# Chunk 0's attention products in halves, and a new written order, in a one-core transformer block

## The chip, the cores and the metric

The kernel runs on one core of a Trainium2 chip. The metric is the device time of one execution in microseconds. A core has five engines that run their own queues side by side: PE (TensorE, matrix products and transposes), DVE (VectorE), ACT (ScalarE), POOL (GpSimd) and SP (SyncE, here only issuing DMAs). POOL and ACT issue DMAs too. Each engine takes its instructions in the order in which the program lists them and waits on semaphores for what other engines or DMAs produce.

## The reference: what is computed

The input x has 2048 positions of 512 values, in bf16. One block is computed:

```python
h = x + A_ref(layernorm(x), wqkv, wo)      # attention
out = h + B_ref(layernorm(h), W_gate, W_up, W_down)   # gated MLP, relu(gate) * up, 1376 wide
```

The attention has 32 heads of 16 values. Each position looks at eight positions only: itself and those 2, 4, ... 14 before it. So for each position and head there are eight scores `q . k / 4`, a softmax over these eight (positions before the start are masked), and a sum of eight `weight * v`. The result goes through `wo`.

## The kernel before, in words

**Chunks.** The 2048 positions are four chunks of 512 (`CS`), named 0 to 3 (`tk`). Data is kept transposed: channels on the 128 partitions, 512 positions along the free side, four tiles of channels (`t` = 0 to 3). A tile named `quad` holds four channel tiles of one chunk (normalized x, q, attention output, normalized h); a tile named `big` holds 8 x 512 values; a `bank` is one of eight accumulators of PE; a `row` is 128 positions of x or h before they are transposed.

**The steps of a chunk.**

1. *Layernorm of x* (lines 397 to 514). DVE takes the statistics (L431, L434), ACT forms the factor with Ln and Exp (L444, L448), DVE normalizes 128 positions at a time into a `row` (L466). The row is transposed by PE (L495) and copied out of the bank by ACT (L511) or, for two rows of chunk 0, by DVE (L509); or, for those in the list `DMAT` (line 348), by a DMA transpose that SP issues (L484). All of chunk 3's x goes that last way.
2. *q, k, v* (lines 529 to 562). Twelve groups of four matmuls (one for each slice of 128 of the contraction), L536, each copied out by ACT (L544). Chunk 0's first four groups (q and k of tiles 0 and 1) are split by positions: the first 256 columns after two transposed rows, the other 256 after the other two.
3. *Scores* (lines 565 to 629). For each half `hf` of the window (four offsets) and each pair of channel tiles, one DVE instruction forms `q * k` for two tiles, four offsets and 512 positions (L583, 128x4096). PE adds up the 16 values of a head with the matrix `sel` (L589, 16 matmuls for each half), ACT takes the exponential (L619), and for chunk 0 DVE masks the start (L622).
4. *Weights* (lines 632 to 697). PE sums the denominators (L639), ACT inverts them by Ln and Exp (L642, L645). In chunks 1 to 3 DVE multiplies the weights by the inverse at once (L663); in chunk 0 the result is divided at the end (L717). The weights are spread over the channels: for chunks 0 and 1 by PE (L689) and eight copies by ACT (L695), for chunks 2 and 3 by eight DMA broadcasts from SP (L679).
5. *Weighted sum* (lines 700 to 751). For each channel tile one DVE instruction forms `weight * v` for all eight offsets (L710, 128x4096). The eight are added in a tree. For chunks 0 to 2 (`DACC`) the first level, four onto four, is an accumulating DMA that POOL issues (L742); the other levels are DVE (L713, 1024 and 512 wide).
6. *Output product and residual* (lines 756 to 782): `wo` on PE (L762); in chunk 0 PE adds x too (L765) and ACT writes the sum (L771), otherwise DVE does it (L773).
7. *Layernorm of h*, with the same helper: squares on ACT (L420), factor on ACT (L441, L448), rows on DVE (L466), transposes.
8. *MLP* (lines 787 to 864): 11 column tiles of up and gate on PE (L800), copied out by ACT (L804, L807), multiplied by DVE (L820), the down product on PE (L837), the last addition on DVE (L848), the store by SP (L854).

**What sets the order.** The kernel does not issue these steps as it walks over the chunks. Each call of `add` (lines 102 to 111) records a step: engine, an estimated duration, what it depends on, which buffers it takes. The list `RANK` (lines 18 to 56) gives each recorded step a number; for each engine the steps go in the order of these numbers (lines 125 to 129). `Plan.order` (lines 116 to 188) places the steps of all engines on one time line with the estimated durations and then issues them by start time, so the estimates decide how engines' steps interleave in the program and which of the shared buffers a step gets, and `RANK` decides the order within an engine. Estimated landing times of the loads are in lines 377 to 379, those of DMA queues in the `dq` of a step (lines 169 to 172).

**The loads** (lines 290 to 321) are not part of the plan and are the same before and after: chunk 0's x, the four slices of the q/k weights (two from SP, two from ACT), chunk 1's x, the v weights, and then the rest.

Of the kernel before, what the change touches and what calls it, by code (L numbers as in the profile page):

```python
# [55 lines left out]
]  # L56


class Op:

# [31 lines left out]
class Plan:  # L92
# [23 lines left out]
    def order(self):  # L116
# [14 lines left out]
        while left:  # L131
# [27 lines left out]
            for eng, cands in best.items():  # L159
# [5 lines left out]
                if pick is None or t < pick[0]:  # L165
                    pick = (t, op)
            t, op = pick
            op.start, op.done = t, t + op.dur + op.lat
            if op.dq:
                at = max(t + op.dur + op.dq[0], free.get("DQ", 0.0)) + op.dq[1]  # L170
                free["DQ"] = at
                op.done = at + op.lat
# [734 lines left out]
```

## Time and profile before

| | |
|---|---|
| time, median of 3 runs | 200.8 us (200.71 to 200.93) |
| the profiled execution's own time | 201.23 us |
| its span, first to last instruction | 199.5 us |
| granted clock of TensorE | 1.000 |
| PE busy | 191.6 us, 96% |
| DVE busy | 152.6 us, 77% |
| ACT busy | 115.0 us, 58% |
| POOL busy | 12.6 us, 6% |

A row of a timeline begins with the start and the length in us from the span's start, then the engine, the line of the kernel, the operation, what is written and read, the shape and a count (x4: four such instructions, merged), and in brackets the idle time of the engine before it and what ended it. A row of the chain of waits has start, length, and what the chain went through. A row of the waits view reads: engine and line, what it waited for, us in total, how often, the longest. A group's row ends with busy us, mean ns of one, and idle us before. A row of the windows view gives, after the stretch, its length and the busy us (and counts) of PE, PE's weight loads, DVE, ACT and POOL, then clock, DMA share and GB/s.

### The profile page before, as it was taken

To read this page: it belongs to the slowest core of one execution; us is meant where nothing else is said; L and a number is where in the kernel's file an instruction comes from. 1 tells how busy PE (TensorE), PEld (TensorE's weight loads), DVE (VectorE), ACT (ScalarE), POOL (GpSimd) and SP (SyncE) were. 2 spreads that over 40 slices of the span, in tenths; PEclk is the share of its full clock that TensorE was granted. 3 is DMA by queue.
4 is the path that set the end of the run, shared out by engine and by line. 5 is a ranking of instruction groups with operands and counts; after the bars stand their busy time and mean duration, and the time that the engine had idled before them with its cause. 6 is when DMAs were issued, how large, how long until landed. Compare 5 with 4: busy or idle time off the path is not lost.

```text
span 199.5 us, 2918 instructions
## 1 busy us (share of the span) xinstructions
PE 191.6 (96%) x1080; PEld 95.7 (48%) x1099; DVE 152.6 (77%) x239; ACT 115.0 (58%) x240; POOL 12.6 (6%) x28
## 2 busy tenths in 40 slices
PE   8599999999999999999999999999999999999994
PEld 8385445554445344444444444444444444444542
DVE  6669999999999999998899859999964423032332
ACT  3455899881999987663844557701439620456500
POOL 4000000330000004100113000000000000000000
PEclk9999999999999999999999999999999999999999
DMA  6959981897000008985269970140010130102022
GB/s 166 327 185 324 412 283 32 156 192 148 3 0 0 3 0 157 190 165 123 39 118 196 208 204 2 26 85 20 3 53 0 26 79 0 31 0 79 0 79 79
DMA packets 19981, 20.92 MB, mean 105 GB/s; under 512 B 8608, under 2 KB 16768, under 8 KB 19968
## 3 DMA queue, kind: packets, MB, share of 16 engines
q1 hardware_dynamic: 17520, 13.60, 23.0%
q0 software_dynamic: 1728, 6.29, 16.8%
q10 hardware_dynamic: 720, 0.85, 1.6%
q8 instruction: 8, 0.13, 0.3%
q14 instruction: 5, 0.04, 0.1%
HBM read 8.42 MB, written 2.10 MB: 53 GB/s over the span
## 4 chain that ended last, share of the span: by engine, by line
PE 91%; DMA 4%; ACT 2%; issue 1%; SPq 1%; DVE 0%
PE bank L800 37%; PE bank L536 21%; PE bank L837 19%; PE bank L762 7%; DMA wqk_sb<-in_A_wqkv_dram 4%; PE bank L589 3%; PE bank L495 2%; ACT big L695 1%; PE bank L639 1%; ACT quad L511 1%; PE bank L765 0%; SPq L292 0%; PE bank L689 0%; ACT quad L544 0%; SPq L294 0%
## 5 line engine op out<-in xcount | busy, mean ns | idle before, releaser
L800 PE MATMUL bank<-quad,wu_sb 128*128 128x512 bf16 (+1 forms) x170 | 42.7, 379 | 0.7 <-ACT quad L511 0.3
L800 PE MATMUL bank<-quad,wg_sb 128*128 128x512 bf16 (+1 forms) x173 | 41.6, 379 | 0.1
L837 PE MATMUL bank<-wd_sb,gT 128*128 128x512 bf16 (+3 forms) x184 | 39.4, 366 | 0.2
L807 ACT ACTIVATE gr<-bank 128x512 bf16<-128x512 f32 (+1 forms) x44 | 25.3, 601 | 23.3 <-PE bank L800 21.8
L804 ACT CAST up_sb<-bank 128x512 bf16<-128x512 f32 (+1 forms) x44 | 25.1, 588 | 23.2 <-PE bank L800 22.4
L710 DVE TENSOR_TENSOR big<-big,vT 128x4096 bf16<-128x4096 bf16 x16 | 36.1, 2290 | 0.8 <-DMA big<-ex 0.6
L583 DVE TENSOR_TENSOR big<-quad,kT 128x4096 bf16<-128x4096 bf16 x16 | 36.2, 2288 | 0.4 <-ACT quad L544 0.4
L536 PE MATMUL bank<-quad,wqk_sb 128*128 128x512 bf16 (+1 forms) x140 | 30.3, 356 | 2.1 <-DMA wqk_sb<-in_A_wqkv_dram 1.8
L820 DVE TENSOR_TENSOR gT<-gr,up_sb 128x1024 bf16<-128x1024 bf16 (+1 forms) x24 | 15.2, 646 | 20.5 <-ACT up_sb L804 10.4
L837 PEld LDWEIGHTS <-gT 128*128 128x128 bf16 (+1 forms) x187 | 18.2, 98 | 19.7
L800 PEld LDWEIGHTS <-wu_sb 128*128 128x128 bf16 (+1 forms) x176 | 17.5, 100 | 21.1 <-issue 1.3
L800 PEld LDWEIGHTS <-wg_sb 128*128 128x128 bf16 (+1 forms) x176 | 17.6, 100 | 20.5 <-issue 0.2
L536 PEld LDWEIGHTS <-wqk_sb 128*128 128x128 bf16 x144 | 15.5, 114 | 14.3 <-DMA wqk_sb<-in_A_wqkv_dram 2.3
L848 DVE TENSOR_TENSOR row<-x_sm,bank 128x512 bf16<-128x512 bf16 (+1 forms) x17 | 10.8, 653 | 10.6 <-PE bank L837 10.6
L713 DVE TENSOR_TENSOR big<-big 128x1024 bf16<-128x1024 bf16 (+2 forms) x24 | 17.2, 735 | 0.7 <-DMA big<-big 0.6
L742 POOL DMA_DIRECT2D big<-big x12 | 10.5, 872 | 86.8 <-DVE big L710 42.7
L536 PE MATMUL bank<-quad,wv_sb 128*128 128x512 bf16 x62 | 15.2, 380 | 0.1
L762 PE MATMUL bank<-wo_sb,quad 128*128 128x512 bf16 x63 | 15.2, 379 | 0.1
L466 DVE TENSOR_SCALAR row<-x_sm,mv,rs 128x512 bf16<-128x512 bf16 x32 | 11.6, 407 | 2.3 <-ACT rs L448 2.1
L431 DVE BATCH_NORM_STATS2 st<-x_sm 128x6 f32<-128x512 bf16 x16 | 10.5, 680 | 3.4 <-DMA x_sm<-in_A_x_dram 3.4
L420 ACT ACTIVATE row<-x_sm,mv 128x512 bf16<-128x512 bf16 x12 | 8.6, 723 | 5.0 <-DVE mv L412 5.0
L544 ACT CAST kT<-bank 128x512 bf16<-128x512 f32 x16 | 9.2, 592 | 3.4 <-PE bank L536 3.4
(68 smaller groups left out, 141.6 us busy)
## 6 DMA issues: line engine op xcount, KB each, us to landing
big<-big POOLq DMA_DIRECT2D x12, 512.0 KB, 5.5
big<-ex SPq DMA_DIRECT2D x16, 128.0 KB, 2.8
out_dram<-row SPq DMA_DIRECT2D x15, 128.0 KB, 1.8
x_sm<-in_A_x_dram SPq DMA_DIRECT2D x3, 512.0 KB, 6.4
wu_sb<-in_B_W_up_dram SPq DMA_DIRECT2D x1, 1376.0 KB, 9.7
wg_sb<-in_B_W_gate_dram SPq DMA_DIRECT2D x1, 1376.0 KB, 12.7
wd_sb<-in_B_W_down_dram SPq DMA_DIRECT2D x1, 1280.0 KB, 15.7
wqk_sb<-in_A_wqkv_dram ACTq DMA_DIRECT2D x2, 256.0 KB, 7.2
```

The lines of the kernel that those rows point to most:

```text
L466: V.tensor_scalar(out=xn.t[:], in0=x, scalar1=mv.t[:, j, 0:1], scalar2=rs.t[:, j:j + 1], op0=ALU.add if residual else ALU.subtract, op1=AL ...
L536: nc.tensor.matmul(mm.t[:, lo:hi], lhsT=wv_sb[:, dt, t:D:NT] if c == 2 else wqk_sb[:, dt, c * D + t:(c + 1) * D:NT], rhs=xnT.t[:, dt, lo:h ...
L583: V.tensor_tensor(out=pb.t[:].rearrange("p (t w) s -> p t w s", t=2), in0=q4, in1=k4, op=ALU.mult)
L710: V.tensor_tensor(out=mt.t[:], in0=ab.t[:], in1=v8, op=ALU.mult)
L713: V.tensor_tensor(out=mt.t[:, 0:n, :], in0=mt.t[:, 0:n, :], in1=mt.t[:, n:2 * n, :], op=ALU.add)
L762: nc.tensor.matmul(od.t[:], lhsT=OT.t[:, t, j * P:(j + 1) * P], rhs=wo_sb[:, t, :], start=(t == 0), stop=(t == NT - 1 and tk not in RPE))
L800: nc.tensor.matmul(mm.t[:fs, :], lhsT=w_sb[:, dt, ft * P: ft * P + fs], rhs=hnT.t[:, dt, :], start=(dt == 0), stop=(dt == NT - 1))
L804: nc.scalar.copy(out=ub.t[:fs, i, :], in_=um.t[:fs, :])
L807: nc.scalar.activation(out=gr.t[:fs, i, :], in_=gm.t[:fs, :], func=ACT.Relu)
L820: V.tensor_tensor(out=gt.t[:fs, 0:n, :], in0=gr.t[:fs, 0:n, :], in1=ub.t[:fs, 0:n, :], op=ALU.mult)
L837: nc.tensor.matmul(od.t[:, c0:c1], lhsT=gts[ft].t[:fs, ft % 2, j * P:(j + 1) * P], rhs=wd_sb[:fs, ft, c0:c1], start=(ft == 0), stop=(ft == ...
L848: V.tensor_tensor(out=ob.t[:, c0:c1], in0=x_sm[:, tk * BPC + j, c0:c1], in1=od.t[:, c0:c1], op=ALU.add)
```

## The change

Five things change in what is issued.

1. **q*k of chunk 0 in halves** (`PRS = (0,)`). Each of the four DVE instructions of L583 becomes two, one for each channel tile (128x2048). Each half depends on the q and k of its own tile alone. PE's sums still come as one step of 16 matmuls after all four halves of a window half.
2. **weight*v of chunk 0 in halves** (`MUH = (0,)`). Each of the four DVE instructions of L710 becomes two, one for each window half; the first depends on the first four weight copies alone. The accumulating DMA still follows both.
3. **The first four q/k groups of chunk 0.** Before: 256 columns, all four slices of the contraction, then the other 256. After: 256 columns with slices 0 and 1, the other 256 with slices 0 and 1, and then all 512 columns with slices 2 and 3. A group is 4 + 2 matmuls in place of 8. The steps on slices 0 and 1 have a load of their own (`ab`) to wait for in the plan.
4. **The plan's estimates.** Later landing times for the loads, and a finer model of DMA queues: accumulating transfers (POOL) share one queue, DMA transposes and broadcasts that meet one of them are planned as slowed.
5. **A new `RANK`**: 735 numbers in place of 722, so the order on every engine is new.

The change's own description adds that chunk 3's DMA transposes are ordered ahead of chunk 0's accumulating transfers. Other options that the code gains (`PRD`, `DAC2`, `HSP`) are empty and issue nothing.

```diff
-    0, 1, 2, 3, 4, 5, ... 720, 721,
+    0, 1, 2, 3, 4, 5, ... 733, 734,
...
+    PRS, MUH = (0,), (0,)
...
-    xload = [[load(t) for t in (3.5, 3.7, 4.1, 4.35)]] + [[load(t)] * BPC for t in (9.15, 13.2, 15.4)]
+    xload = [[load(t) for t in (3.5, 3.7, 4.1, 4.35)]] + [[load(t)] * BPC for t in (10.8, 14.4, 17.8)]
...
-             (("q", 7.78), ("k", 7.78), ("v", 10.6), ("o", 17.1), ("u", 20.5), ("g", 24.0), ("d", 28.5))}
+             (("q", 9.55), ("k", 9.55), ("ab", 8.1), ("v", 12.1), ("o", 19.2), ("u", 22.6), ("g", 26.1), ("d", 30.1))}
...
-                a = None
+                ab, done = [wload["ab"]], []
                 for i, (lo, hi, evs) in enumerate(((0, 2 * P, xev[0:2]), (2 * P, CS, xev[2:]))):
-                    a = add(("qk%s%d" % ("ac"[i], n), tk), "PE", 4 * MM * (hi - lo) / CS + 0.02,
-                            lambda f=f_mm, lo=lo, hi=hi: f(lo, hi), evs + [wl, a, fills[-1]], pr - 5, take=[mm],
-                            use=[xnT], lat=PEL if i == 1 else 0.0)
+                    done.append(add(("qk%s%d" % ("ac"[i], n), tk), "PE", 2 * MM * (hi - lo) / CS + 0.005,
+                                    lambda f=f_mm, lo=lo, hi=hi: f(lo, hi, 0, 2), evs + ab + done + [fills[-1]], pr - 5,
+                                    take=[mm], use=[xnT]))
+                a = add(("qkd%d" % n, tk), "PE", 2 * MM, lambda f=f_mm: f(0, CS, 2, NT), done + [wl], pr - 4.9, take=[mm],
+                        use=[xnT], lat=PEL)
...
+                if tk in PRS:
+                    def f_p1(u, t=t, hf=hf, pb=pb, qT=qT, s0=s0):
+                        kb = kT[:, t + u, PADL + s0 - 4 * hf * DIL: PADL + s0 - 4 * hf * DIL + CS]
+                        k4 = bass.AP(tensor=kb.tensor, offset=kb.offset,
+                                     ap=[list(kb.ap[0]), [-DIL, 4]] + [list(y) for y in kb.ap[1:]])
+                        V.tensor_tensor(out=pb.t[:, 4 * u:4 * u + 4, :],
+                                        in0=qT.t[:, t + u, :].unsqueeze(1).to_broadcast([P, 4, CS]), in1=k4, op=ALU.mult)
+
+                    for u in range(2):
+                        a = add(("pr%d%s" % (hf, "ac"[u]), tk), "DVE", D20, lambda u=u, f=f_p1: f(u),
+                                [d[t + u] for d in (qd, kd, kp)], apr, take=[pb], use=[qT], lat=DL)
+                        prd.append((a, pb, f_sc if u else lambda: None))
...
+            if tk in MUH:
+                def f_m1(hf, t=t, ab=ab, mt=mt, s0=s0):
+                    vb = vT[:, t, PADL + s0 - 4 * hf * DIL: PADL + s0 - 4 * hf * DIL + CS]
+                    v4 = bass.AP(tensor=vb.tensor, offset=vb.offset,
+                                 ap=[list(vb.ap[0]), [-DIL, 4]] + [list(y) for y in vb.ap[1:]])
+                    V.tensor_tensor(out=mt.t[:, 4 * hf:4 * hf + 4, :], in0=ab.t[:, 4 * hf:4 * hf + 4, :], in1=v4, op=ALU.mult)
+
+                ms = [add(("mu%d%s" % (t, "ac"[hf]), tk), "DVE", D20, lambda hf=hf, f=f_m1: f(hf),
+                          [x for x in abd if x.key[0][2] == str(hf)] + vds, tpr, take=[mt], use=[ab], lat=DL) for hf in range(2)]
```

More of the change, by code (lines that the diff above doesn't have):

```diff
@@ L168, in order @@
             op.start, op.done = t, t + op.dur + op.lat
+            held = 0.0
             if op.dq:
-                at = max(t + op.dur + op.dq[0], free.get("DQ", 0.0)) + op.dq[1]
-                free["DQ"] = at
+                at, sw, busy = t + op.dur + op.dq[0], free.get("DQ", 0.0), op.dq[1]
+                if op.eng == "POOL":
+                    late = 1.0 if at < free.get("DT", -1.0) + 0.3 else 0.0
+                    at = free["DQ"] = max(at, sw) + late + busy
+                else:
+                    turn = 0.6 < busy < 0.9
+                    at = max(at, free.get("DQ" + op.eng, 0.0))
+                    if at < sw + (0.3 if turn else 0.0):
+                        share = 0.03 if turn else 0.18
+                        late = max(sw - at, 0.0)
+                        at += busy / share if late * share >= busy else late + busy - late * share
+                        free["DQ"] = sw + (1.65 if turn else 0.5 * busy)
+                        held = at + op.lat - 4.5
+                    else:
+                        at += busy
+                    free["DQ" + op.eng] = at
+                    if turn:
+                        free["DT"] = at
                 op.done = at + op.lat
-            free[op.eng] = t + op.dur
+            free[op.eng] = max(t + op.dur, held)
             for b in op.take:
@@ L216 @@
     PRE = ()
+    PRD = ()
     NAB = 0
@@ L532, with f_mm @@
             pr = base + 10 + 0.1 * n
-            def f_mm(lo=0, hi=CS, c=c, t=t, mm=mm, xnT=xnT):
-                for dt in range(NT):
+            def f_mm(lo=0, hi=CS, d0=0, d1=NT, c=c, t=t, mm=mm, xnT=xnT):
+                for dt in range(d0, d1):
                     nc.tensor.matmul(mm.t[:, lo:hi], lhsT=wv_sb[:, dt, t:D:NT] if c == 2 else wqk_sb[:, dt, c * D + t:(c + 1) * D:NT],
-                                     rhs=xnT.t[:, dt, lo:hi], start=(dt == 0), stop=(dt == NT - 1))
+                                     rhs=xnT.t[:, dt, lo:hi], start=(dt == 0 and lo == 0), stop=(dt == NT - 1))
             def f_ev(c=c, t=t, mm=mm, qT=qT, s0=s0):
@@ new lines, with f_pd, f_sc @@
+            if (tk, hf) in PRD:
+                def f_pd(p0=prd[0][1], p1=prd[1][1]):
+                    nc.gpsimd.dma_start(p0.t[:], p1.t[:], accum_op=ALU.add, max_dma_last_dim=4096)
+                a = add(("pd%d" % hf, tk), "POOL", 1.3, f_pd, [a for a, _, _ in prd], apr, use=[b for _, b, _ in prd],
+                        lat=1.1, dq=(0.75, 5.48))
+                def f_sc(sc=sc, pb=prd[0][1]):
+                    for u in range(2):
+                        for g in range(4):
+                            nc.tensor.matmul(sc.t[g * HB:(g + 1) * HB, :], lhsT=sel[:],
+                                             rhs=pb.t[:, 4 * u + g, :], start=(u == 0),
+                                             stop=(u == 1), tile_position=(0, g * HB))
+                scd = [add(("sc%d" % hf, tk), "PE", 2 * MM + SW, f_sc, [a], apr, take=[sc], use=[prd[0][1]], lat=PEL)]
+            elif (tk, hf) in PRE:
@@ L796, with f_mm @@
                 pr = mb + ft * 0.1
[L798 removed]
+                def f_mm(w_sb, mm, lo=0, hi=CS, ft=ft, fs=fs, hnT=hnT):
                     for dt in range(NT):
[L800 to L801 removed]
+                        nc.tensor.matmul(mm.t[:fs, lo:hi], lhsT=w_sb[:, dt, ft * P: ft * P + fs],
+                                         rhs=hnT.t[:, dt, lo:hi], start=(dt == 0), stop=(dt == NT - 1))
                 def f_ue(um=um, ub=ub, fs=fs, i=ft - f0):
```

48 lines of the change are left out of this document (31 added, 17 removed), and 74 rows, old and new, of the table RANK.

## The prediction

> **What bounds the kernel now.** I read the page first (busy shares, slices), then TensorE's waits, the chain that ended last, and the timelines of TensorE (PE) and VectorE (DVE) around the two places where PE stood still.
>
> ```profile
> span 199.5 us, 2918 instructions
> PE 191.6 (96%) x1080; PEld 95.7 (48%) x1099; DVE 152.6 (77%) x239; ACT 115.0 (58%) x240; POOL 12.6 (6%) x28
> PE   8599999999999999999999999999999999999994
> DVE  6669999999999999998899859999964423032332
> ...
> PE bank L536 <- DMA wqk_sb<-in_A_wqkv_dram: 1.8, 2, 1.0
> ...
> PE bank L800 <- ACT quad L511: 0.3, 1, 0.3
> ```
>
> PE is busy in all slices but the first and last. DVE is full from the fourth slice to the twentieth (15 to about 95 us) and half idle later. So the end is PE's amount of work plus the little that PE stands still. Two waits carry names: 1.8 us at the start for the q/k weights, and 0.3 us for `quad` of L511, the normalized chunk 0 that the gated MLP reads.
>
> ```profile
> 8.66 0.41 PE L536 MATMUL bank<-quad,wqk_sb 128*128 128x256 bf16 x2 [0.85 <-DMA wqk_sb<-in_A_wqkv_dram]
> 10.05 0.85 PE L536 MATMUL bank<-quad,wqk_sb 128*128 128x256 bf16 x6 [0.98 <-DMA wqk_sb<-in_A_wqkv_dram]
> ...
> 66.88 1.02 PE L800 MATMUL bank<-quad,wu_sb 128*128 128x512 bf16 x3 [0.27 <-ACT quad L511]
> ```
> ```profile
> 10.89 0.45 PE bank L495 x8
> ...
> 24.79 0.33 PE bank L689 x4
> ...
> 57.70 0.98 PE bank L589 x16
> ...
> 69.33 5.34 PE bank L800 x24
> ...
> 196.55 0.42 DVE row L848
> ```
>
> PE starts at 8.66 with the first two weight slices, stops 0.98 us for the other two, and then runs to 196.55, where the tail begins (0.42 of DVE and the last store). At 66.88 PE has run out of everything that does not need chunk 0's normalized residual. That point is **the gate**: whatever PE gains before it counts only if the gate opens earlier too. The gate is opened by DVE:
>
> ```profile
> 11.15 0.69 DVE L431 BATCH_NORM_STATS2 st<-x_sm 128x6 f32<-128x512 bf16 x1 [2.80 <-DMA x_sm<-in_A_x_dram]
> 11.76 0.41 DVE L509 COPY quad<-bank 128x512 bf16<-128x512 bf16 x1
> ...
> 14.74 0.69 DVE L431 BATCH_NORM_STATS2 st<-x_sm 128x6 f32<-128x512 bf16 x1 [0.30 <-DMA x_sm<-in_A_x_dram]
> ...
> 43.07 2.29 DVE L583 TENSOR_TENSOR big<-quad,kT 128x4096 bf16<-128x4096 bf16 x1 [0.37 <-ACT quad L544]
> ...
> 63.35 1.38 DVE L466 TENSOR_SCALAR row<-x_sm,mv,rs 128x512 bf16<-128x512 bf16 x4
> ```
> ```profile
> 11.15:63.35 52.20, 51.88 (x322) 27.18 (x326) 51.30 (x71) 41.58 (x90) 3.76 (x5) 1.00 0.59 163
> ```
>
> From the landing of chunk 1's x at 11.15 to the four row normalizations at 63.35 (the third figure after the stretch's length is DVE) DVE works 51.30 of 52.20 us. Its queue up to those rows sets the gate.
>
> **The change part by part.** Halves touch chunk 0 alone; the new ranks move everything, so I count what stands ahead of two places in the built order.
>
> *Start of PE.* The q/k products of four banks now run their first two weight slices for all banks before the last two, and the eight row transposes at 10.89 (0.45) go ahead of 8.66, into the 0.85 us wait. The 0.98 us stop is filled by such products. Thirty-two 256-wide matmuls become sixteen and eight 512-wide ones: same columns, taken as equal. Head start: 0.98 + 0.45 = 1.43 us. A new wait may eat into it: v's first product moves up behind 16 half and 8 whole q/k matmuls, which at 0.85/6 and 5.34/24 us take at most 4.05 us, and 3.56 with a half at half of a whole one, so it is reached between 12.2 and 12.7.
>
> ```profile
> 3.85 0.44 SPq L310 DMA_DIRECT2D wv_sb<-in_A_wqkv_dram  x1
> wv_sb<-in_A_wqkv_dram SPq DMA_DIRECT2D x1, 512.0 KB, 8.6
> ```
>
> The weights land at 3.85 + 8.6 = 12.45: a wait of 0 to 0.25 us, with q/k products queued behind it. It costs nothing as long as PE still arrives early at the gate, which it does, below.
>
> *DVE up to the gate.* The prices:
>
> ```profile
> 35.41 6.69 DVE L710 TENSOR_TENSOR big<-big,vT 128x4096 bf16<-128x4096 bf16 x3
> 64.63 0.76 DVE L663 TENSOR_TENSOR ex<-ex,rec 128x512 bf16<-128x512 bf16 x2
> ```
> ```profile
> L583 DVE TENSOR_TENSOR big<-quad,kT 128x4096 bf16<-128x4096 bf16 x16 | 36.2, 2288 | 0.4 <-ACT quad L544 0.4
> ...
> L713 DVE TENSOR_TENSOR big<-big 128x2048 bf16<-128x2048 bf16 x4 | 4.9, 1222 | 0.1
> ```
>
> Three whole products in a row take 6.69, one alone 2.29, so each advances the queue by 2.20 and 0.09 of its duration lies beside its neighbour. A half is not in the trace; the nearest row is the 2048-wide add, 1222 ns, so 1.13 in the queue, and a pair costs 2.27 against 2.20: 0.07 more, eight pairs 0.56. The ends: nothing (a pair is a whole), or no overlap at all, 2 x 1222 - 2288 = 156 ns a pair, 1.25 in all. I take 0.56, since every run of products in the rows overlaps.
>
> [...]
>
> The order: ahead of chunk 0's four hidden rows there stand now eight whole k products of chunks 1 to 3 instead of seven (+2.20), and one `ex*rec` more (0.76 for two: +0.38). The copy at 11.76 moves ahead of 11.15 (0.41 less an overlap of 0.09: -0.32). The waits of 0.30 and 0.37 have instructions with inputs long there in their places now (-0.67). Sum: 63.35 + 0.56 + 2.20 + 0.38 - 0.32 - 0.67 = **65.50** for the first hidden row. The extra product is not lost (a later one is spared), but it stands ahead of the gate.
>
> The rows also need ACT's normalization factor:
>
> ```profile
> 53.39 0.86 PE bank L762 x4
> ```
> ```profile
> 51.43 0.75 DVE L717 TENSOR_TENSOR quad<-big,rec 128x512 bf16<-128x512 bf16 x2
> ...
> 54.50 0.61 ACT L771 ACTIVATE x_sm<-bank 128x512 bf16<-128x512 f32 x1
> 62.15 0.22 ACT L448 ACTIVATE rs<-rs 128x4 f32<-128x4 f32 x1
> ```
>
> Chunk 0's attention output was complete at 52.18. In the after four whole k products stand ahead of it, not two: 52.18 + 4.40 + 0.56 - 0.32 - 0.67 = 56.15. The output product begins there (PE is waiting) and reaches ACT 1.11 later, as from 53.39 to 54.50: 57.3. From there ACT took 7.87 to the factor (62.37), with five other instructions among the squares and residuals; now there are five again: 65.2. PE has 1.3 us of other work among the four output products now, which may cost some tenths. So the factor comes just ahead of DVE; I add nothing, and keep 0.3 for the range.
>
> *From the rows to the gate.*
>
> ```profile
> 5.59 0.40 PE L495 MATMUL bank<-identity,row 128*128 128x128 bf16 x4
> ...
> 6.03 0.59 ACT L511 COPY quad<-bank 128x512 bf16<-128x512 bf16 x1 [0.23 <-PE bank L495]
> ```
> ```profile
> 64.90 1.93 ACT L511 COPY quad<-bank 128x1024 bf16<-128x1024 bf16 x2
> ```
>
> Two of the four rows take about 0.7 (1.38 for four): the second ends at 66.2. Four transposes and the way to ACT take 6.03 - 5.59 = 0.44: ACT begins at 66.7, with 0.05 from DVE to PE, needs 1.93 for both copies, and PE starts 0.05 later (66.83 to 66.88 before): **68.67**. PE is early: before, it began the transposes at 64.42;
>
> ```profile
> 64.42 0.46 PE bank L495 x8
> ```
>
> now 1.43 less, and 0.98 + 0.33 more, because one more pair of k-score groups (57.70) and one more broadcast (24.79) stand ahead of them: 64.3, or 64.55 with the v wait. The first row is there at 65.9. So the whole head start ends in 1.3 to 1.6 us of waiting on DVE.
>
> *After the gate.* Before, PE took 196.55 - 66.88 = 129.67 from there. The after has 1.31 of that done (0.98 + 0.33), and 0.19 was a wait ahead of 69.33 (the broadcast before it began at 68.81, 0.33):
>
> ```profile
> 68.81 0.40 PE L689 MATMUL bank<-ex,spread 32*128 32x512 bf16 x4
> ```
>
> SP keeps eight broadcasts, two hidden transposes, eight broadcasts in this sequence; one output store slides behind the second eight, and nothing waits for a store but its row buffer. I cost that, and the other moves past the gate, at nothing. Left: 128.17. End of PE: 68.67 + 128.17 = 196.84, against 196.55: +0.29. The gate breaks even at 68.38. The profiled execution took 201.23 for its span of 199.5, 0.43 above the median of the runs, 200.8; the same difference on the median gives **201.1 us**. The halves of weight*v are inside the sum; that they begin with four of eight weights gains nothing, because DVE is full there.
>
> **The rivals.** A measurement here tells about 0.2% from no change: 200.4 to 201.2 counts as the same.
>
> *Faster: the head start survives.* If DVE's queue were some 1.7 shorter than my sum, the gate would open when PE arrives and 1.43 would stay: 200.8 - 1.43 = 199.4. For it: the stop of 0.98 is real. Against it: the queue is counted, not guessed, and bounds of the halves move it by 0.56 at most, to 200.5.
>
> *Slower: chunk 0's first accumulating transfer is late.* The first tree add waits for it. By its queue DVE issues the first weight*v half at 32.2 (32.88 before, one row, the copy and the 0.30 less, four pairs of halves more), ends the pair with a row between at 34.9, and reaches the add five half products and a row later, at 40.8.
>
> ```profile
> 32.88 2.28 DVE L710 TENSOR_TENSOR big<-big,vT 128x4096 bf16<-128x4096 bf16 x1
> 35.76 1.01 POOL L742 DMA_DIRECT2D big<-big  x1 [24.41 <-DVE row L466]
> DMA to landing us min/median/max: 5.2/6.2/7.0
> ```
>
> The transfer starts 0.60 after its product's end (35.16 to 35.76), so at 35.5, and lands at 40.7 if it takes 5.2, the shortest in chunk 0. From 5.3 us on, each further microsecond delays DVE, the gate and the end alike: at 6.2 +0.9, 202.0; at 7.0 +1.7, 202.8. The title's order is at stake here: the first three transposes of chunk 3 stand ahead of the first weight*v product before and after, but the fourth row is normalized one half product after the first pair, so its transpose still goes out with the transfer under way, as before (of four issued from 32.18 the longest landed in 5.3, the others in 2.5). So the change does not do all that it says.
>
> ```profile
> 32.18 5.23 SPq L484 DMA_TRANSPOSE quad<-row  x4
> DMA to landing us min/median/max: 2.5/2.5/5.3
> ```
>
> *Slower: halves at full price.* Without overlap the pairs cost 1.25, 0.69 more: 201.8. The rows of three products in 6.69 us speak against it. [...]
>
> **How the numbers follow.** Forecast 0.50, own range 200.5 to 201.5 (halves from nothing on the low side, ACT's factor 0.3 late on the high), of which 0.43 lies within 0.2% and 0.07 above. Faster 0.12. Late transfer 0.24. Full price 0.14. So faster 0.12, same 0.43, slower 0.45. The range of 8 in 10 leaves out the faster case and the late transfer's far end: 200.4 to 202.2.
>
> **What would show it.** Right: q/k products without the 0.98 stop; hidden rows of chunk 0 near 65.5 with DVE full before; PE waiting 1.3 to 1.6 us for rows ahead of the chunk 0 transposes; the first gate product near 68.7 and 128.2 from there to PE's end. Wrong: rows before 65.0 or after 66.0, a DMA named ahead of the first tree add, half products spaced other than 1.13 apart, or named PE waits after the gate, which I cost at nothing because ACT and DVE have room there (DVE's slices fall to 4 and 2).

## The result, and the profile after

The changed kernel takes **200.45 us** (median of 20 runs, 200.30 to 200.57) where the kernel before takes 200.85 (20 runs, 199.63 to 202.80). The ratio is 0.9983, 95% interval 0.9975 to 0.9992: 0.17% faster, where the prediction had 201.1, 0.3 us slower. That is inside the 0.2% that it called the same and inside its range, but in the other direction. Repeated on another occasion the ratio was 0.9985 (0.9975 to 0.9995), so the small gain is there both times. The runs of the changed kernel also lie much closer together.

Here is the page of the changed kernel and its TensorE waits (line: us in total, times, longest).

```profile
span 198.8 us, 2949 instructions
...
PE 192.4 (97%) x1091; PEld 94.5 (48%) x1091; DVE 153.2 (77%) x247; ACT 116.0 (58%) x240; POOL 12.7 (6%) x28
...
PE   8799999999998999999999999999999999999994
...
DVE  5799999999999999999999689999861230121714
```
```profile
PE bank L516 <- DVE row L487: 2.3, 4, 0.9
```

The wait for q/k weights and that for `quad` have left the list. What is left is TensorE waiting for rows that DVE normalizes (L487, L466 before). Its timeline shows where:

```profile
8.81 3.64 PE L557 MATMUL bank<-quad,wqk_sb 128*128 128x256 bf16 x24
12.28 1.03 PE L557 MATMUL bank<-quad,wv_sb 128*128 128x512 bf16 x4
...
64.99 1.37 PE L516 MATMUL bank<-identity,row 128*128 128x128 bf16 x16 [0.90 <-DVE row L487]
...
67.76 1.02 PE L869 MATMUL bank<-quad,wg_sb 128*128 128x512 bf16 x4
```

The q/k products (L557) run from 8.81 without a stop, v has no wait at 12.28, and 0.90 us is lost at the hidden rows of chunk 0. The gate (L869, L800 before) opens at 67.76. DVE up to there:

```profile
9.98 2.47 DVE L452 BATCH_NORM_STATS2 st<-x_sm 128x6 f32<-128x512 bf16 x4 [1.13 <-DMA x_sm<-in_A_x_dram]
...
18.57 0.69 DVE L452 BATCH_NORM_STATS2 st<-x_sm 128x6 f32<-128x512 bf16 x1
...
19.54 3.50 DVE L621 TENSOR_TENSOR big<-quad,kT 128x2048 bf16<-128x2048 bf16 x3 [0.20 <-ACT kT L565]
...
29.03 0.24 DVE L455 BATCH_NORM_AGGREGATE mv<-st 128x2 f32<-128x6 f32 x2
...
35.15 4.63 DVE L777 TENSOR_TENSOR big<-big,vT 128x2048 bf16<-128x2048 bf16 x4
39.70 0.69 DVE L765 TENSOR_TENSOR big<-big 128x1024 bf16<-128x1024 bf16 x1
...
64.53 1.38 DVE L487 TENSOR_SCALAR row<-x_sm,mv,rs 128x512 bf16<-128x512 bf16 x4
```

Two things differ from the forecast. Chunk 1's x was there at 9.98, not 11.15, though nothing in its load changed; and the hidden rows came at 64.53, not 65.50; the prediction had named rows before 65.0 as a sign that it is wrong. From the gate to the last addition it is then as forecast, 195.85 - 67.76 = 128.09 (128.17 predicted). So the error lies ahead of the gate, and the questions are what belongs to the landing, what to DVE's queue, and whether that queue is the bound at all.

### The profile page after: what moved, and what is told of

Read it like the earlier page. It is cut to its first block, busy times and chain, and to the rows that moved or that the text cites. A ratio compares the mean times of both kernels' runs of the same rounds, so it can differ in the third digit from the quotient of the medians.

```text
span 198.8 us, 2949 instructions
## 1 busy us (share of the span) xinstructions
PE 192.4 (97%) x1091; PEld 94.5 (48%) x1091; DVE 153.2 (77%) x247; ACT 116.0 (58%) x240; POOL 12.7 (6%) x28
## 4 chain that ended last, share of the span: by engine, by line
PE 88%; ACT 5%; DVE 2%; DMA 1%; issue 1%
PE bank L869 38%; PE bank L557 20%; PE bank L914 19%; PE bank L831 6%; PE bank L612 3%; DMA x_sm<-in_A_x_dram 1%; PE bank L516 1%; DVE st L452 1%; ACT row L441 1%; ACT x_sm L840 1%; ACT big L747 1%; ACT quad L532 1%; PE bank L690 1%; ACT vT L565 0%; DVE row L487 0%
## 5 line engine op out<-in xcount | busy, mean ns | idle before, releaser
L869 PE MATMUL bank<-quad,wg_sb 128*128 128x512 bf16 (+1 forms) x176 | 42.9, 379 | 0.1
L869 PE MATMUL bank<-quad,wu_sb 128*128 128x512 bf16 (+1 forms) x176 | 42.6, 379 | 0.0
L914 PE MATMUL bank<-wd_sb,gT 128*128 128x512 bf16 (+3 forms) x187 | 40.2, 366 | 0.0
L557 PE MATMUL bank<-quad,wqk_sb 128*128 128x512 bf16 (+1 forms) x136 | 30.3, 367 | 0.0
L869 PEld LDWEIGHTS <-wg_sb 128*128 128x128 bf16 (+1 forms) x176 | 17.5, 100 | 20.7 <-issue 0.7
L869 PEld LDWEIGHTS <-wu_sb 128*128 128x128 bf16 (+1 forms) x176 | 17.6, 100 | 20.4
L762 DVE TENSOR_TENSOR big<-big,vT 128x4096 bf16<-128x4096 bf16 x12 | 27.1, 2286 | 0.2 <-issue 0.2
L606 DVE TENSOR_TENSOR big<-quad,kT 128x4096 bf16<-128x4096 bf16 x12 | 27.2, 2284 | 0.0
L557 PEld LDWEIGHTS <-wqk_sb 128*128 128x128 bf16 x136 | 14.8, 114 | 11.7 <-issue 1.1
L557 PE MATMUL bank<-quad,wv_sb 128*128 128x512 bf16 x64 | 15.5, 380 | 0.0
L487 DVE TENSOR_SCALAR row<-x_sm,mv,rs 128x512 bf16<-128x512 bf16 x32 | 11.5, 406 | 1.4 <-ACT rs L469 1.4
L565 ACT CAST vT<-bank 128x512 bf16<-128x512 f32 x16 | 9.4, 605 | 4.1 <-PE bank L557 4.1
L565 ACT CAST quad<-bank 128x512 bf16<-128x512 f32 x16 | 9.4, 607 | 3.9 <-PE bank L557 3.9
```

Source lines behind the costliest of these rows:

```text
L557: nc.tensor.matmul(mm.t[:, lo:hi], lhsT=wv_sb[:, dt, t:D:NT] if c == 2 else wqk_sb[:, dt, c * D + t:(c + 1) * D:NT], rhs=xnT.t[:, dt, lo:h ...
L565: nc.scalar.copy(out=o, in_=mm.t[:])
L606: V.tensor_tensor(out=pb.t[:].rearrange("p (t w) s -> p t w s", t=2), in0=q4, in1=k4, op=ALU.mult)
L762: V.tensor_tensor(out=mt.t[:], in0=ab.t[:], in1=v8, op=ALU.mult)
L869: nc.tensor.matmul(mm.t[:fs, lo:hi], lhsT=w_sb[:, dt, ft * P: ft * P + fs], rhs=hnT.t[:, dt, lo:hi], start=(dt == 0), stop=(dt == NT - 1))
L914: nc.tensor.matmul(od.t[:, c0:c1], lhsT=gts[ft].t[:fs, ft % 2, j * P:(j + 1) * P], rhs=wd_sb[:fs, ft, c0:c1], start=(ft == 0), stop=(ft == ...
```

## The experiments

### The landing: both kernels again, and x loaded later

No edit for the first two.

> The kernel before, unchanged, profiled a second time, to see what of its profile belongs to the program. In the first profile chunk 1's x landed at 11.15, the gate (the first gated-MLP product that needs chunk 0) opened at 66.88, 55.73 later, and that execution took 201.23. Theory A (the landing differs from execution to execution and the gate follows it one for one): the landing differs from 11.15 by some tenths, gate minus landing is again 55.4 to 56.0, and the profiled time differs from 201.23 by what the landing differs. Theory B (the late landing belongs to the program before, the early one to the changed program): 11.0 to 11.3 again, gate at 66.7 to 67.1, 201.0 to 201.4.

> The changed kernel, unchanged, profiled a second time. In the first profile chunk 1's x landed at 9.98 and the gate opened at 67.76, 57.78 later. Theory A: the landing may be anywhere from 9.5 to 11.5, gate minus landing 57.5 to 58.1 (less if the landing is so early that the first half product waits for ACT's copy of k instead), and the time goes with it. Theory B: 9.9 to 10.1 again, gate at 67.6 to 67.9. Median of the timed runs 200.3 to 200.6 under both.

DVE's timeline (to the last addition), and TensorE's from its last wait ahead of the gate to the first gate product, the kernel before again:

```profile
10.74 0.69 DVE L431 BATCH_NORM_STATS2 st<-x_sm 128x6 f32<-128x512 bf16 x1 [2.34 <-DMA x_sm<-in_A_x_dram]
...
62.94 1.38 DVE L466 TENSOR_SCALAR row<-x_sm,mv,rs 128x512 bf16<-128x512 bf16 x4
...
196.15 0.42 DVE L848 TENSOR_TENSOR row<-x_sm,bank 128x256 bf16<-128x256 bf16 x1 [0.52 <-PE bank L837]
```
```profile
11.82 5.39 PE L536 MATMUL bank<-quad,wqk_sb 128*128 128x256 bf16 x31 [0.27 <-DVE quad L509]
...
63.85 1.06 PE L495 MATMUL bank<-identity,row 128*128 128x128 bf16 x16
...
66.47 1.02 PE L800 MATMUL bank<-quad,wu_sb 128*128 128x512 bf16 x3 [0.27 <-ACT quad L511]
```

The changed kernel again, DVE and TensorE:

```profile
10.76 2.47 DVE L452 BATCH_NORM_STATS2 st<-x_sm 128x6 f32<-128x512 bf16 x4 [1.99 <-DMA x_sm<-in_A_x_dram]
...
19.36 0.69 DVE L452 BATCH_NORM_STATS2 st<-x_sm 128x6 f32<-128x512 bf16 x1
...
20.04 3.46 DVE L621 TENSOR_TENSOR big<-quad,kT 128x2048 bf16<-128x2048 bf16 x3
...
29.07 0.24 DVE L455 BATCH_NORM_AGGREGATE mv<-st 128x2 f32<-128x6 f32 x2
...
64.45 1.37 DVE L487 TENSOR_SCALAR row<-x_sm,mv,rs 128x512 bf16<-128x512 bf16 x4
...
195.78 0.42 DVE L925 TENSOR_TENSOR row<-x_sm,bank 128x256 bf16<-128x256 bf16 x1 [0.24 <-PE bank L914]
```
```profile
8.73 3.64 PE L557 MATMUL bank<-quad,wqk_sb 128*128 128x256 bf16 x23
...
67.69 1.02 PE L869 MATMUL bank<-quad,wg_sb 128*128 128x512 bf16 x3
```

The kernel before took 200.78 (11 runs), its profiled execution 200.82: landing 0.41 earlier than in the first profile, gate 0.41 earlier, time 0.41 shorter, gate minus landing 55.73 both times. Theory A holds for it. The changed kernel took 200.48 (12 runs) and behaves otherwise: the landing is 0.78 later than in its first profile and the gate 0.07 *earlier*. The two DVE timelines show where the 0.78 goes: still there at 18.57 against 19.36, smaller behind the half products at 19.54 and 20.04 (which waited 0.20 for ACT's copy of k in the one and not in the other), and 0.04 at 29.03 against 29.07. Theory A had allowed for that wait only with a landing earlier still, B not at all. Fifteen profiled executions here have this load unchanged: it landed from 9.94 to 11.15, the median 10.60. The profile on which the prediction was built had the latest landing of all.

The load was then moved on purpose, in both kernels:

```diff
-        nc.sync.dma_start(x_sm[:, BPC:2 * BPC, :], x_rows[:, BPC:2 * BPC, :])
...
         nc.sync.dma_start(wv_sb[:], w3_r[:, :, 2 * D:3 * D])
+        nc.sync.dma_start(x_sm[:, BPC:2 * BPC, :], x_rows[:, BPC:2 * BPC, :])
```

> The kernel before, its load of chunk 1's x issued behind the load of wv instead of ahead of it, so that it lands about 1 us later. Both theories agree here: the copy of chunk 0's last transposes stands behind chunk 1's first statistic on DVE, and q/k products wait for that copy, so gate and time go with the landing one for one: gate minus landing 55.5 to 56.0, time 200.8 plus what the landing is behind 10.74, about 201.8.

> The changed kernel with the same edit. Theory of the prediction (DVE's queue runs unbroken from the landing to the rows, so it shifts one for one): time 200.45 plus the whole shift, as much as the kernel before loses. Theory C (in the changed kernel the queue is held later by ACT, at the first half that waits for kT and at the two masks, so a landing up to about 10.8 costs nothing, and only what lies beyond counts): a landing at 11.8 gives rows at 65.4 to 65.6, gate 68.6 to 68.8 and 201.4; gate minus landing falls from 57.8 (landing 9.98) to 56.9 (10.76 and later).

Before: 201.89 (5 runs; ratio 1.0069, 1.0045 to 1.0093), gate minus landing 66.97 - 11.24 = 55.73 once more (the profiled execution, 201.32, was the shortest of the five). After: 201.39 (10 runs; ratio to the kernel before 1.0036, 1.0020 to 1.0053); its DVE:

```profile
11.56 2.47 DVE L452 BATCH_NORM_STATS2 st<-x_sm 128x6 f32<-128x512 bf16 x4 [2.80 <-DMA x_sm<-in_A_x_dram]
...
65.18 1.37 DVE L487 TENSOR_SCALAR row<-x_sm,mv,rs 128x512 bf16<-128x512 bf16 x4
```

In the after, 0.80 of landing (10.76 to 11.56) moves the rows by 0.73, where 0.78 (9.98 to 10.76) moved them by -0.08. Theory C holds: it expected 201.4 and a gate 56.9 behind the landing (it is 68.41 - 11.56 = 56.85). The changed kernel has a floor at a landing of about 10.8, and the kernel before has none in the range seen. An estimate from the two profiles: the lines cross where 200.82 + landing - 10.74 is 200.46, at 10.38, and with x earlier than that the kernel before would be the faster one.

### The start of TensorE, and what ties it to the landing

The moves in the kernel before, shown as the built order: the split of the q/k groups as in the change, the transposes and the copy ahead; the last pair of lines is only in the third kernel.

```diff
 PE
+xtp2 xtp3 (8 row transposes)
 q/k products of chunk 0
-xtp2 xtp3
 DVE
+copy of chunk 0's transposes
 statistic of chunk 1
-copy of chunk 0's transposes
...
-statistic of chunk 2
 first q*k product
+statistic of chunk 2
```

> The kernel before with the start of the change alone: four q/k groups take weight slices 0 and 1 first, the last two row transposes and the copy go ahead of them; whole products, and the rest of the order as before. The prediction's theory (DVE's queue sets the gate): the head start of 1.43 us on TensorE ends in waiting for the rows; only the copy moved ahead of the wait for x shortens DVE's queue, by 0.3, so 200.5 to 200.85 against 200.85. Rival (the head start survives): 1.4 us less, 199.4.

> The kernel before with two moves alone: chunk 0's last two row transposes ahead of the first q/k products on TensorE, and the copy of one of them ahead of chunk 1's first statistic on DVE, so that it no longer stands behind the landing of chunk 1's x; the q/k products as before. TensorE's wait for the copy (0.27) goes and 0.3 of DVE's queue; the stop for weights (0.87) stays: 200.4 to 200.6. If what ties the kernel before to the landing is this copy, the timed runs spread less than before's (200.3 to 201.0 in eleven runs); if it is the statistic of chunk 2, as much.

> The kernel before with the start of the change, and chunk 2's first statistic moved behind the first q*k product, which takes out the wait of 0.58 for that load ahead of the product. If DVE's queue alone sets the gate: rows and gate 0.58 earlier than with the start alone, 200.0. If TensorE's own queue is the bound there (it stood still for only 0.27 us between 18.3 and the gate): no more than those 0.27 and the 0.25 at 18.3, 200.0 to 200.5.

| | median | ratio to before | runs from, to | gate minus landing |
|---|---|---|---|---|
| head start | 200.56 (12) | 0.9994 (0.9979 to 1.0008) | 200.13, 201.15 | 65.76 - 10.50 = 55.26 |
| copy and transposes ahead | 200.65 (12) | 0.9998 (0.9978 to 1.0019) | 199.87, 201.71 | 65.97 - 10.64 = 55.33 |
| head start, statistic later | **199.78** (9) | 0.9958 (0.9943 to 0.9973) | 199.50, 199.93 | 65.54 - 10.98 = 54.56 |

The head start alone is worth 0.5 us of gate, near the 0.3 of the prediction's theory and far from 1.4, and in the time neither of the first two can be told from no change. TensorE starts early and then meets a wait further on (the first of the three):

```profile
18.28 0.62 PE L495 MATMUL bank<-identity,row 128*128 128x128 bf16 x8 [0.25 <-DVE row L466]
```

Those rows are chunk 1's; they stand on DVE behind the first q*k product, and that behind chunk 2's first statistic, which waits for a load that is issued only when chunk 1's x is there (L313 on SyncE waits 7.0 us for that in the kernel before; the statistic waits 0.30 to 0.80 us in the seven profiles of the kernel before and its variants that keep this order). With the statistic moved the ratio falls by a further 0.0036, some 0.7 us, which the intervals do not tell from the 0.5 to 0.6 of the two expectations. The gate itself moved by 0.22 only (65.76 to 65.54), as TensorE's bound has it, but it did so with the landing 0.48 later, and the runs close up from a spread of 1 us to 0.43. Moving the copy alone leaves them wide apart, so once the copy is out of the way it is this statistic that carries the landing into the time. The changed kernel has the same statistic behind its first half product (with no wait there). That this is why its runs are even was not tried in it by itself; the three rows of the table and the two late loads agree with it. The third kernel is the fastest one here and has whole products throughout.

### The halves

In the order of before, each pair in the place of its whole (`PRS, MUH = (0,), (0,)`, rest unchanged):

> The kernel before with chunk 0's products in halves, each pair at the place of its whole product; nothing else. The prediction's theory (0.07 us a pair in the queue, 8 pairs): gate and time +0.56, 201.4. Full price (156 ns a pair): +1.25, 202.1. Free halves: 200.85.

200.68 (11 runs), ratio 1.0000 (0.9988 to 1.0013); gate minus landing 66.09 - 10.35 = 55.74 against 55.73. Neither the 202.1 of the full price nor the 201.4 of 0.56 appeared. The single durations do show the full price: a weight*v half lasts 1217 ns here, a whole 2283 in the kernel before again, and 2 x 1217 - 2283 = 151 ns, near the 156 of the prediction. The queue does not: counted from start to next start, the sixteen halves take 18.13 us of it, where eight wholes at 2.20 take 17.60. That is 0.53, near the 0.56 of the prediction and far from 1.25. The time shows none of it, and so does not tell the two prices apart by itself. From the landing to the rows DVE is busy 0.36 us more than in the kernel before, and a wait of 0.37 for ACT ahead of a later product is gone, so the rows come 0.11 later; and TensorE, which takes the first row 0.4 after it is there (63.06 and 63.47; 63.34 and 63.85 in the kernel before again), does not notice:

```profile
10.35:62.66 52.31, 51.56 (x317) 26.89 (x322) 51.58 (x79) 41.35 (x90) 3.78 (x5) 1.00 0.58 164
```
```profile
10.74:62.94 52.20, 51.62 (x318) 26.93 (x322) 51.22 (x71) 41.31 (x90) 3.77 (x5) 1.00 0.59 164
```

(Third figure after the length: DVE; the first row is the halves, the second the kernel before again.)

In the new order each kind of half was undone by itself, the whole product in the place of its later half:

```diff
-    PRS, MUH = (0,), (0,)
+    PRS, MUH = (0,), ()
```

and `(), (0,)` for the other.

> The changed kernel with chunk 0's weight*v products whole again, each at the place of its later half; q*k stays in halves. Theory of the prediction (the halves only cost, 0.28 us for four pairs, and that they begin with four of eight weights gains nothing): rows 0.3 earlier, 200.2. Theory D (the first half, at 31.1, starts ahead of ACT's last broadcast copies, which end at 32.1; a whole product has to wait for them): DVE idles 0.7 to 0.8 ahead of the first product, saves 0.3 later, rows 0.4 to 0.5 later, 200.9.

> The changed kernel with chunk 0's q*k products whole again, each at the place of its later half; weight*v stays in halves. Theory of the prediction (halves only cost): rows 0.2 to 0.3 earlier, 200.2. Theory D (in the new order the first three halves need only the first of two tiles of q and k; a whole product has to wait for the second tile's copy, which ends at 19.5): DVE stands still for about 2.5 us ahead of 19.5, which comes back in part; rows 2.0 to 2.6 later, 202.4 to 203.1.

Whole weight*v: 201.81 (6 runs; 1.0062, 1.0043 to 1.0081), by the medians 1.36 slower than the change. Whole q*k: 202.94 (4 runs; 1.0107, 1.0081 to 1.0132), 2.5 slower. DVE's timelines, first the one, then the other:

```profile
31.34 0.41 DVE L487 TENSOR_SCALAR row<-x_sm,mv,rs 128x512 bf16<-128x512 bf16 x1 [0.34 <-PE bank L516]
32.01 2.29 DVE L762 TENSOR_TENSOR big<-big,vT 128x4096 bf16<-128x4096 bf16 x1 [0.25 <-ACT big L747]
...
39.89 0.69 DVE L765 TENSOR_TENSOR big<-big 128x1024 bf16<-128x1024 bf16 x1 [0.87 <-DMA big<-big]
...
65.61 1.38 DVE L487 TENSOR_SCALAR row<-x_sm,mv,rs 128x512 bf16<-128x512 bf16 x4
```
```profile
19.34 2.29 DVE L606 TENSOR_TENSOR big<-quad,kT 128x4096 bf16<-128x4096 bf16 x1 [1.94 <-ACT kT L565]
...
66.84 1.37 DVE L487 TENSOR_SCALAR row<-x_sm,mv,rs 128x512 bf16<-128x512 bf16 x4
```

Theory D has the right sign in both, and for q*k the size too; for weight*v it had only the first two waits (0.59), and missed the third, 0.87 at the first tree add. TensorE, whose next products then come late, waits 1.25 for DVE at 48.11 in the first kernel and reaches the gate at 68.84, and in the other at 70.07, against 67.69 in the changed kernel again. The 0.87 is the prediction's slower rival, the late accumulating transfer, met here and not in the change, whose transfer has these two rows (start and length; median to landing):

```profile
34.37 1.01 POOL L805 DMA_DIRECT2D big<-big  x1 [24.18 <-DVE big L777]
```
```profile
big<-big POOLq DMA_DIRECT2D x1, 512.0 KB, 5.0
```

It lands at 39.4 and the tree add follows at 39.70, 0.3 us to spare. As forecast, the fourth transpose of chunk 3 still goes out with it under way (at 35.3, between 34.37 and 39.4), so the named order is kept for three of four.

### Is DVE's queue the bound?

The prediction said that its queue sets the gate, since DVE works 51.30 of 52.20 us. One whole product, 2.20 us, was taken out ahead of the rows, in each kernel:

```diff
+                    if (tk, hf, t) == (1, 0, 0):
+                        return
                     V.tensor_tensor(out=pb.t[:].rearrange("p (t w) s -> p t w s", t=2),
```

> The kernel before without chunk 1's first q*k product (the sums that read it read the second product's buffer instead, so chunk 1's scores are not the reference's): 2.20 us less of DVE's queue ahead of the gate. Theory of the prediction (DVE's queue sets the gate): rows 1.2 to 2.2 earlier (the tree adds may wait for their transfers instead), and the gate with them until TensorE itself is the bound. Theory P (TensorE is full up to the gate in the kernel before, 0.27 us of standing still aside): at most 0.3 to 0.4 less, 200.3 to 200.5, however much earlier the rows are.

> The changed kernel without the same product (chunk 1's scores are not the reference's). Here TensorE stood still for 0.90 us ahead of the rows. DVE's queue as the bound of the gate, with the head start hidden under it: TensorE's wait of 0.90 goes and the time falls by 0.8 to 1.0, 199.5 to 199.7, less than the 2.2 taken out, since TensorE is the bound from there. If the head start were not hidden under DVE: no change, 200.45.

Neither time moved: 200.68 (12 runs; ratio 0.9995, 0.9981 to 1.0010) and 200.38 (12 runs; 0.9984, 0.9968 to 0.9999, against 0.9985 for the change itself). Theory P (TensorE is full up to the gate) fits the time of the first. It allowed for rows that come early, but they did not even do that (62.03 - 9.94 = 52.09 from the landing, 52.20 with the product). In the second my forecast of 0.9 less failed altogether. DVE's waits in the two kernels:

```profile
43.20 0.69 DVE L717 TENSOR_TENSOR big<-big 128x1024 bf16<-128x1024 bf16 x1 [1.09 <-DMA big<-big]
48.40 1.15 DVE L717 TENSOR_TENSOR big<-big 128x1024 bf16<-128x1024 bf16 x2 [0.36 <-DMA big<-big]
55.17 0.21 DVE L412 TENSOR_SCALAR mv<-sm 128x1 f32<-128x1 f32 x2 [0.55 <-ACT x_sm L775]
62.03 1.38 DVE L466 TENSOR_SCALAR row<-x_sm,mv,rs 128x512 bf16<-128x512 bf16 x4
```
```profile
46.50 1.36 DVE L769 TENSOR_TENSOR big<-big 128x1024 bf16<-128x1024 bf16 x3 [1.48 <-DMA big<-big]
56.94 0.15 DVE L433 TENSOR_SCALAR mv<-sm 128x1 f32<-128x1 f32 x1 [0.52 <-ACT x_sm L844]
64.30 1.38 DVE L487 TENSOR_SCALAR row<-x_sm,mv,rs 128x512 bf16<-128x512 bf16 x4
```

1.09 + 0.36 + 0.55 = 2.00 of the 2.20 come back as waits for accumulating transfers and for ACT's residual; 1.48 + 0.52 = 2.00 in the other. A second chain stood right behind the queue. To find where it ends, three more, with a product taken out behind the transfers, the other chain shortened, and both:

```diff
 (1)  chunk 3's first q*k product left out, as above with (3, 0, 0)
 (2)  PE   -v product of chunk 3   wo of chunk 0, last   +v product of chunk 3
      ACT  -2 weight copies, 1 copy of v   factor   +2 weight copies, 1 copy of v
```

> The changed kernel without chunk 3's first q*k product, which stands between chunk 0's statistics and its hidden rows on DVE (the sums read the other product's buffer, so chunk 3's scores are not the reference's). DVE's queue alone as the bound: rows 2.2 earlier until TensorE's wait of 0.90 is used up, 199.5 to 199.7. Theory F (two chains end within 0.1 us of each other: DVE's queue at 64.45, and TensorE's output products, ACT's squares and the normalization factor at 64.37): rows no earlier than the factor, which gains at most 0.4 from the earlier statistics: 200.0 to 200.4.

> The changed kernel, nothing left out, with only the other chain shortened: one v product goes behind chunk 0's last output product on TensorE, and two broadcast copies and one copy of v go behind the normalization factor on ACT. Theory F: the factor comes 0.4 to 1.8 earlier, the rows stay where DVE's queue has them, 200.35 to 200.5. If ACT's chain alone were the bound: the rows follow the factor, 199.6 to 200.0.

> Both edits at once (chunk 3's scores are not the reference's). Theory F: both chains are shorter now, the rows come at 62.3 to 63.2, TensorE's wait of 0.90 ahead of them goes, and TensorE is the bound: 199.5 to 199.7. If something else holds TensorE there (the hidden head start is not to be had this way): 200.0 or more.

Without the product: 200.42 (12 runs; 0.9998, 0.9987 to 1.0010, against runs of before that had a median of 200.50 on that occasion), so no change again, as theory F has it, and the factor is there at 64.19, just ahead of the rows. But DVE's own queue got no shorter either:

```profile
58.65 0.15 DVE L433 TENSOR_SCALAR mv<-sm 128x1 f32<-128x1 f32 x1 [1.50 <-ACT x_sm L844]
59.17 0.42 DVE L718 TENSOR_TENSOR ex<-ex,rec 128x512 bf16<-128x512 bf16 x1 [0.37 <-ACT rec L700]
59.74 0.15 DVE L433 TENSOR_SCALAR mv<-sm 128x1 f32<-128x1 f32 x1 [0.15 <-ACT x_sm L844]
64.28 1.38 DVE L487 TENSOR_SCALAR row<-x_sm,mv,rs 128x512 bf16<-128x512 bf16 x4
```

The 2.2 us come back as 1.50 + 0.37 + 0.15 of waiting ahead of the small statistics of the residuals (L433) and of the inverse, which ACT delivers one by one behind TensorE's output products; the two products behind the third statistic then lead to the rows at the same place. That is a third chain, over TensorE, ACT and DVE in turn, that theory F did not have. In the other two kernels the rows stayed where they were too, though the factor was there at 63.8 and 63.7: at 64.53 with DVE's queue full, and at 64.45 with 1.57 of waiting ahead of the same statistic. Both kernels were slower, 201.34 (6 runs; 1.0040, 1.0025 to 1.0055) and 201.27 (6 runs; 1.0040, 1.0025 to 1.0056): the three copies, once behind the factor, stand ahead of the copies of the transposed rows, and TensorE waits for those (the last kernel):

```profile
68.51 1.02 PE L873 MATMUL bank<-quad,wg_sb 128*128 128x512 bf16 x3 [0.55 <-ACT quad L532]
```

So that edit brought a wait of its own, and whether TensorE's hidden 0.90 us can be had by shortening all three chains stays open.

The traces say more about the bound than theories P and F do. Here is TensorE in the changed kernel without chunk 1's product:

```profile
8.58 3.64 PE L557 MATMUL bank<-quad,wqk_sb 128*128 128x256 bf16 x24
...
64.77 1.36 PE L516 MATMUL bank<-identity,row 128*128 128x128 bf16 x16 [0.90 <-DVE row L487]
...
67.54 1.02 PE L873 MATMUL bank<-quad,wg_sb 128*128 128x512 bf16 x4
```

Its wait for the rows is 0.90, as with the product. The gate stands at a fixed distance behind the point from which TensorE no longer waits for another engine, but for those 0.90 in the changed kernel and for ACT at the gate itself (0.1 there, 0.27 in the kernel before):

| kernels | that point | gate | distance |
|---|---|---|---|
| changed: first profile, again, without chunk 1's product, without chunk 3's | 8.81, 8.73, 8.58, 8.55 | 67.76, 67.69, 67.54, 67.51 | 58.95 to 58.96 |
| before: again, x late, halves, a product less | 11.82, 12.31, 11.42, 11.02 | 66.47, 66.97, 66.09, 65.75 | 54.65 to 54.73 |
| head start, copy ahead, statistic later | 18.28, 18.48, 18.06 | 65.76, 65.97, 65.54 | 47.48 to 47.49 |

The work of DVE differs by 2.2 us inside the first two groups, and the landing by 0.8 and 1.3, yet the distance moves by less than 0.1. So in both kernels it is TensorE's own queue that leads to the gate, and DVE's queue counts where it makes TensorE wait: in the kernel before at the copy of chunk 0's transposes (L509, 1.1 behind the landing), in the changed kernel over the third chain. There the hidden rows follow TensorE's first output product of chunk 0 by 9.37 to 9.38 in all nine executions, and this loop returns to TensorE 0.90 too late. At a landing of about 10.8 DVE's queue ends together with it; a later x holds TensorE itself: with x loaded late DVE begins chunk 1's first row at 15.35 (13.76 in the first profile, where TensorE takes such rows at 15.30). No run shortened that loop.

## Why the prediction was wrong, point by point

*The head start: right in kind.* No stop for weights, no wait for v, and TensorE loses it again ahead of the rows: 0.90 where 1.3 to 1.6 were forecast. (In the kernel before the transposes of those rows began at 64.25; the row at 64.42 that the prediction quotes is eight of the sixteen.)

***The step that failed: the sum to 65.50 for the first hidden row.*** At an equal landing (10.74 before, 10.76 after) DVE takes 53.69 from landing to rows, where the sum 52.20 + 0.56 + 2.20 + 0.38 - 0.32 - 0.67 gives 54.35: 0.66 too much, which carries over to the end, 195.78 after against 196.15 before, -0.37 where +0.29 was forecast. Two terms were mis-sized and one was put at nothing. DVE's idle time fell by 0.85, from 52.20 - 51.22 = 0.98 to 53.69 - 53.56 = 0.13, where the sum took away 0.67: that is 0.18 of the 0.66. The halves cost 0.46 (sixteen take 18.06 of the queue), not 0.56: 0.10. The remaining 0.38 lies in instructions that both kernels have in equal number, and that follow each other more closely in the new order (the statistics with their aggregates take 8.09 in place of 8.32, the row normalizations 3.85 in place of 3.94, the 1024-wide tree adds 2.41 in place of 2.56; the 512-wide ones 0.07 more). The sum counted them as unchanged without a reason. Why the new order spaces them so was not tried. The whole product, the `ex*rec` and the copy came as forecast, within 0.03. The window of the changed kernel again:

```profile
10.76:64.45 53.69, 52.82 (x327) 26.12 (x331) 53.56 (x79) 43.04 (x93) 3.80 (x5) 1.00 0.56 159
```

The halves in rows: four of weight*v advance the queue by 39.70 - 35.15 = 4.55, 0.07 a pair as forecast, two of q*k (16.33 to 18.57) by 2.24, 0.04.

*What stood behind that step ("Its queue up to those rows sets the gate") was wrong too.* A queue that works 98% of a stretch was read as the bound of that stretch, starting at one landing. Longer queues do move the gate, by making TensorE wait (x late in the changed kernel: gate 68.41 against 67.69; the whole products: 68.84 and 70.07); shorter ones do not (a product less moves the rows by 0.1 to 0.2 of 2.2 us). In the kernel before, DVE's queue was not the bound at all: the rows lay ready 0.5 before TensorE took the first. And the start is not the landing: in the change ACT holds DVE at 19.54 (0.20) and again before 29 (its exponential ends at 28.92, the mask on DVE follows at 28.95), so up to a landing of 10.8 the landing does not count. In the kernel before it counts in full, over the copy that TensorE waits for, and the prediction used one execution of it, the latest of fifteen. That its sum came within 0.66 at all is luck in part: at that landing the queue that it counts happens to end within 0.1 of the chain that sets the rows. Because the forecast was made as a difference on that same execution, the landing by itself did not falsify it.

*From rows to gate and to the end: right.* 67.76 - 64.53 = 3.23 (3.17 forecast), 128.09 (128.17).

*"That they begin with four of eight weights gains nothing, because DVE is full there": wrong.* In the new order it is worth about 1.4 us, through waits that come back when it is taken away.

*The rivals.* The faster one (the head start survives, 199.4) did not come; the gain of 0.37 between the two repeated profiles is the forecast loss of 0.29 less the 0.66 of the sum. The late transfer did not come, with 0.3 us to spare. The full price of halves is refuted by their spacing in the queue in both orders, 0.53 and 0.46 in place of 1.25.

## What to carry to other kernels

An engine that is busy in 98% of a stretch is not yet its bound (here 51.30 of 52.20 us, and 2.2 us of work less moved neither time): ask what would wait if one piece were taken out, and try it with that piece left out. Look too whether the engine on which the end depends ever waits for that queue; where its starts keep a fixed distance from execution to execution, as the gate here (58.95 to 58.96 us), its own queue is the bound to look at. When an edit reorders a full queue, the instructions that it does not change can be spaced differently (0.38 us here); price them by start to next start, and count the idle time as length less busy time, not only the waits that carry a name. And profile a kernel more than once before a difference of 0.2% is worked out from it: look which event, here a load's landing (9.94 to 11.15), differs between executions, and whether each version hangs on it.

## What the runs showed of the hardware

- The same load at the same place in the queues landed between 9.94 and 11.15 us in fifteen executions: 1.2 us, against a gain of 0.3 to 0.4 to be measured.
- 2.2 us of work taken out of a full queue of DVE came back as 2.0 us of waiting in three kernels.
- TensorE's gate product stood 58.95 to 58.96 us behind its first q/k product in four executions of the changed kernel, though the landing of chunk 1's x differed by 0.8 us and two of them had 2.2 us less work on DVE.
- Two 128x2048 products in place of one 128x4096 take 0.04 to 0.07 us more of DVE's queue, though the single durations of a pair add up to 0.13 more for q*k (2 x 1204 - 2281 ns) and 0.15 for weight*v.
